# A new instruction list for an attention-and-MLP block: first loads on two queues, segment 0's Q and K in the space of w2 and hT, steps of VectorE on GpSimd

## The chip, the core and the metric

The kernel runs on one core of a Trainium2 chip. The core has TensorE (PE, matmuls), VectorE (DVE), ScalarE (ACT), GpSimd (POOL) and SyncE (SP), each with its own instruction stream executed in order, and 16 DMA engines that are fed by queues of SP and of ACT. Times are microseconds on the device. The metric is the time of one execution; the profile's span runs from its first to its last instruction.

## The reference

One layer on x of 2048 tokens by 640: attention with a compressive memory, then an MLP, each behind a layer norm and with a residual. All inputs are bfloat16.

```python
q, k, v = (heads(layernorm(x) @ w) for w in (wq, wk, wv))      # 32 heads of 20
for s in range(4):                                             # segments of 512 tokens
    p = softmax(q_s @ k_s.T * 20**-0.5 + causal_mask)
    a_dot = p @ v_s
    a_mem = (phi(q_s) @ M) / (phi(q_s) @ z + 1e-6)             # phi(t) = t + 1 if t > 0 else exp(t)
    o_s = sigmoid(beta) * a_mem + (1 - sigmoid(beta)) * a_dot
    M, z = M + phi(k_s).T @ v_s, z + sum(phi(k_s))
h = x + concat(o) @ wo
out = h + silu(layernorm(h) @ w1) @ w2                         # hidden width 1728
```

## The kernel before

**Tiling.** Tokens lie in 16 blocks of 128, four to a segment. A segment goes through these steps, named as in the list below; s is the segment, b the block, c a column group of five, g one of eight groups of four heads.

- `n1_st b` (DVE): mean and variance of a block, two statistics instructions and one aggregate (L711, L714). `n1_ra`, `n1_rb` (POOL): add epsilon (L720), power -0.5 (L725). `n1_ap` (DVE): subtract and multiply (L732) into one of four buffers `xn`. In segment 0 PE transposes it (`n1_tp`, L741) and ACT copies it (`n1_te`, L750); later segments use a transposing DMA (`n1_tr`, L756). `n2_...` is the same for the second norm.
- `v s i` (PE, L783) and `ve` (ACT or DVE): V of a block. `pr s c w` (PE, L817) and `qe`: a projection to Q (w=0) or K (w=1) and its copy into the tile `QK`. `re_wq c`, `re_wk c` rearrange the columns of wq and wk first (L682 on ACT, L684 on DVE). `vt` (SP, L857): 12 small DMAs that gather the last heads from `QK` into `QKV` (the virtual heads, groups 5 to 7). `ex`, `pha`, `phb`: phi of Q and K.
- `qk` (PE, L893), `e` (ACT, L904: the exponential, 768 or 1024 elements at a time), `mk` (POOL, L915: the causal mask on a diagonal part), `av` (PE, L936), `oe`, `tn`, `nm`, `ad`: scores, softmax and output of a group. In segment 0 each group is done in halves: `x` for its first two blocks, `ya` and `yb` for the last two.
- `kt` (transposing DMA), `mz`, `ma`, `mb`: the memory. `ot`, `wo` (PE, L1119), `rs`: output projection and residual.
- `h1` (PE, L1153; its last tile of 64 columns L1148), `th` (ACT, L1162), `s` (DVE, L1168), `h2` (PE, L1195), `o` (DVE, L1208): the MLP.
- `fill N` (PE, L604): N matmuls on a zero tile whose result nothing reads.

**Order.** Nothing is scheduled on the chip. A string `ORDER` lists every step by name, with the PSUM banks and buffers that it takes (`:4`) and, where there is a choice, its engine (`/A` ACT, `/D` DVE, `/G` POOL). The program emits the steps in that order, so each engine's stream is the list reduced to that engine. A tracker (`Tracker`) adds the semaphore waits that reads and writes need. An instruction whose input is late holds up all that stand behind it on its engine. Eight PSUM banks are shared; a `qk` takes four.

**Loads.** SP issues nearly all DMAs. x0 to x3 are the four blocks of segment 0; x4, x8 and x12 load four blocks each for the later segments. wq and wk go to the space of the MLP's tile `sT`. In the list x8 comes after the first `vt`. Each segment writes the same tiles `QK`, `QKV` and `xT`, so that segment 1's projections wait for segment 0's scores.

Of the kernel before, what the change touches and what calls it, by code (L numbers as in the profile page):

```python
# [6 lines left out]
ALU = mybir.AluOpType  # L7
# [340 lines left out]
SPLIT0 = ()  # L348
WH = [(0, 0), (0, 1), (1, 0), (1, 1)]
# [33 lines left out]
mk6yb_256 qk7ya0:4 th0_0_0:0 s0_7_0:0 tn4y:0 h1_0_8_0:3 e7ya0:2 nm4y:3 mz01:1 s0_0_0 mz04:0 e7ya2 ma01/D:2 phb101 kt10:0
kt03:1 h1_0_3_0:2 ma04/D:1 tn5y:1 th0_8_0:1 qk7yb0:4 th0_3_0:0 s0_8_0 av6y:0 e7yb0:0 s0_3_0 h1_0_1_0:3 nm5y:1 e7yb2
h1_0_12_0:2 th0_1_0:1 mk7yb_0 qk8a0:4 th0_12_0:0 pr110:1 e8a2:1 s0_12_0 s0_1_0 mm0 mk7yb_256 e8a0 mzc0 h1_0_10_0:2
qe110/D av7y:3 th0_10_0:1 vt19:0 qk8e0:4 s0_10_0 pr130:1 e8e2:0 vt16 oe6y/D:1 w_w2_3 n1_ap10:2 oe7y/D:0 e8e0 h1_0_5_0:2
pha121:0 qe130/D:0 w_w2_0 h1_0_11_0:3 th0_5_0:1 mk8e_0 qk8b0:4 s0_5_0 th0_11_0:0 tn7y:0 h1_0_6_0:1 e8b0:6 nm7y:3 mz03:2
ma03/D:4 s0_11_0 e8b2 h1_0_2_0:0 pha100:0 n1_ap8:1 h1_0_13_0:2 pha120:0 th0_2_0:1 qk9a0:4 mk8b_0 th0_13_0:0 pr131:3
s0_13_0 e9a2:4 mk8a_0 s0_2_0 mk8b_384 e9a0 h1_0_4_0:0 qe131/D n1_tr8:0 mk8e_256 h1_0_9_0:2 pha141:2 th0_6_0:1 mm3
th0_4_0:0 qk9b0:4 s0_6_0 mzc4 mzc6 ex100:1 mk9a_0 vt17 av8:3 s0_4_0 th0_9_0:1 mzc3 pha110:0 e9b2:3 h2_0_0:0 mm2 phb100  # L390
phb121 s0_9_0 mm9 pha111:1 mtb2 vt18 vt110 mzc9 mm8 e9b0 mm11 h2_0_1 oe8/D:0 mzc5 n1_tr10 ex141:1 mk9b_0 mm10 qk10a0:4
tn6y:3 h2_0_2 e10a2:5 phb141 mm1 vt11 nm6y:0 mzc2 n1_rb9 h2_0_3 e10a0 vt13 mb01:0 mm7 vt111 mzc1 qk10b0:4 mk9b_384 o0
h2_1_0:2 e10b2:2 ot3 mb00:0 e10b0 tn8:0 h2_1_1 n1_tr11 ex120:0 mk10b_0 nm8:2,1 qk10e0:4 ex111:1 h2_1_2 vt15 mk10b_384
phb111 n1_ap9:0 e10e2:1 mk10a_0 vt14 av9:0 e10e0 phb120 ot2 h2_1_3 oe9/A:0 ex110:0 mk10e_0 mk10e_256 qk11a0:4 kt12:1 o1
wo3:0 e11a0:6 pha130:0 mb02:0 phb110 e11a2 vt10 av10:2 rs3 n1_tr9 ex131:0 qk11b0:4 mk11a_0 oe10/D:1 tn9:0 e11b0:2
nm9:1,0 vt12 wo2:2 e11b2 ex130:1 mk11b_0 qk12a0:4 rs2 v20:0 e12a2:4 n2_st2:7 mzc7 e12a0 mzc8 mk11b_384 av11:2 pha131:0
n2_st3:1 ve20/A:1 qk13a0:4 mz12:3 e13a0:2 e13a2 v21:0 ma12 kt11:1 n2_ra3 phb130 n2_rb3 mzc11 mz10:3 n2_ra2 mzc10 ve21/A
n2_rb2 qk12b0:4 ma10 n2_ap3:1 ad8:0 e12b0:6 tn10:0 n2_tr3 pr210:3 nm10:0,1 mk13a_0 e12b2 mb03:0 qe210/A:0 ad9 qk12e0:4
oe11/D:1 pr220:0 e12e0:0 phb131 mk12b_0 n2_ap2:2 kt13:0 e12e2 mk12b_384 pr231:1 pha140:0 mk12a_0 qe220/A:0 n2_tr2
mk12e_0 qk13b0:4 qe231/D:0 tn11:2 e13b2:5 pr200:0 mk12e_256 nm11:3,0 ad10 e13b0 av12:1 qe200/D:0 mk13b_0 qk14a0:4 v23:2  # L400
e14a2:1 phb140 mk13b_384 oe12/D:1 mb04:0 e14a0 av13:1 ve23/A qk14b0:4 mz13:0 e14b2:3 pr221:2 ma13 oe13/D:0 e14b0
h1_0_7_1:3 qe221/A mk14b_0 qk14e0:4 th0_7_1:1 tn13:0 s0_7_1 mk14a_0 pr211:2 nm13:3,1 mk14b_384 e14e0:0 e14e2 h1_0_8_1:3
qe211/D mk14e_0 qk15a0:4 th0_8_1:1 pr241:0 e15a0:4 s0_8_1 mk14e_256 ad11 e15a2 av14:2 qe241/D:0 ad13 mz11:1 oe14/A:0
qk15b0:4 ma11 mk15a_0 e15b0:1 tn14:2 h1_0_4_1:1 nm14:3,1 e15b2 pr201:0 th0_4_1:1 mk15b_0 tn12:4 s0_4_1 qe201/A
h1_0_12_1:7 nm12:0,0 mk15b_384 qk16b0:0 e16b0:2 th0_12_1:0 ad14 av15:6 h1_0_13_1:4 ad12 oe15/D:0 e16b2 pr240:5 pha200:0
s0_12_1 th0_13_1:1 pha210:0 pha211:0 tn15:6 s0_13_1 qe240/A ex210:0 qk16a0:0 nm15:0,0 pr230:4 e16a2:6 e16a0 h1_0_10_1:5
# [54 lines left out]
def build(nc, es, A_x, A_wq, A_wk, A_wv, A_wo, A_beta, B_x, B_w1, B_w2, out):  # L461
# [229 lines left out]
    for c in range(NC):  # L691
        load_w(f"w1_{c}", w1_sb[:, c, :], B_w1[128 * c:128 * c + 128, :], -1 + 0.2 * c, 1.4, [(W["w1"], [c])])
# [172 lines left out]
    def declare_ticks(s):  # L865
# [5 lines left out]
        def operands(g, sub=WH):  # L871
            if g < 5:
                return (qk[g], sub), QK[:, g, 0, :], QK[:, g, 1, :]
# [395 lines left out]
```

## Time and profile before

| | |
|---|---|
| timed runs | 305.26, 305.55, 305.59 us; median 305.55 |
| profiled execution, first to last instruction | 303.6 us |
| median of the runs less that span | 1.95 us |
| PE, DVE, ACT, POOL busy | 294.4, 214.4, 226.6, 141.7 us |
| first V matmul starts | 9.03 us |
| first scores, first exponential (segment 0) | 16.33, 16.72 us |
| last scores of segment 0 | 67.47 us |
| DMA | 24.65 MB, mean 81 GB/s |

The profile's page gives busy time by engine, the span in 40 slices, the DMA queues, the chain that ended last, and the costliest groups of instructions; the trace adds timelines, waits and busy time by windows. In rows of groups the columns are line, engine, operation, output and input tiles with shapes, count, busy time, mean ns of one, and the idle time before them with what ended it. A line such as L711 is that line of the program before; the changed program's lines lie a few further on.

### The profile page before, as it was taken

To read this page: it belongs to the slowest core of one execution; us is meant where nothing else is said; L and a number is where in the kernel's file an instruction comes from. 1 tells how busy PE (TensorE), PEld (TensorE's weight loads), DVE (VectorE), ACT (ScalarE), POOL (GpSimd) and SP (SyncE) were. 2 spreads that over 40 slices of the span, in tenths; PEclk is the share of its full clock that TensorE was granted. 3 is DMA by queue.
4 is the path that set the end of the run, shared out by engine and by line. 5 is a ranking of instruction groups with operands and counts; after the bars stand their busy time and mean duration, and the time that the engine had idled before them with its cause. 6 is when DMAs were issued, how large, how long until landed. Compare 5 with 4: busy or idle time off the path is not lost.

```text
span 303.6 us, 7334 instructions
## 1 busy us (share of the span) xinstructions
PE 294.4 (97%) x2934; PEld 167.9 (55%) x2934; DVE 214.4 (71%) x492; ACT 226.6 (75%) x321; POOL 141.7 (47%) x280
## 2 busy tenths in 40 slices
PE   6999989999999999999999999999999999999996
PEld 5634545466565455566643545556564466764565
DVE  4888967877868866958588975858847494835623
ACT  3689988999999999899889989968779951004500
POOL 3346574532875856546847317564564730400000
PEclk9999999999999999999999999999999999999999
DMA  6938375843544130063551300043241006221003
GB/s 211 363 104 159 69 153 87 272 37 77 166 87 75 39 42 2 2 122 69 106 154 42 67 19 0 2 89 69 56 97 36 2 0 89 43 66 66 0 3 107
DMA packets 48721, 24.65 MB, mean 81 GB/s; under 512 B 39152, under 2 KB 47600, under 8 KB 48688
## 3 DMA queue, kind: packets, MB, share of 16 engines
q1 hardware_dynamic: 48400, 23.86, 34.6%
q8 instruction: 23, 0.38, 0.5%
q10 hardware_dynamic: 288, 0.33, 0.4%
q14 instruction: 10, 0.08, 0.1%
HBM read 10.41 MB, written 2.62 MB: 43 GB/s over the span
## 4 chain that ended last, share of the span: by engine, by line
PE 72%; ACT 12%; DVE 7%; DMA 4%; SPq 2%; issue 1%; POOL 0%; ACTq 0%
PE ps_all L1195 17%; PE ps_all L1153 13%; PE ps_all L817 13%; ACT PT L904 8%; PE ps_all L893 7%; PE ps_all L1119 6%; PE ps_all L783 5%; PE ps_all L936 5%; DVE sT L1168 3%; DMA wv_sb<-in_A_wv_dram 2%; ACT th L1162 2%; PE ps_all L965 2%; PE ps_all L1058 2%; DMA x_tok<-in_A_x_dram 1%; PE ps_all L969 1%
## 5 line engine op out<-in xcount | busy, mean ns | idle before, releaser
L904 ACT ACTIVATE PT<-ps_all 128x1024 bf16<-128x1024 f32 (+1 forms) x168 | 156.3, 985 | 16.9 <-PE ps_all L893 15.9
L915 POOL TENSOR_SCALAR_AFFINE_SELECT PT<-PT 128x512 bf16<-128x512 bf16 x128 | 81.5, 650 | 52.8 <-ACT PT L904 51.5
L1195 PE MATMUL ps_all<-w_sb,sT 128*128 128x320 bf16 (+2 forms) x462 | 64.8, 295 | 0.1
L1153 PE MATMUL ps_all<-hT,w_sb 128*128 128x512 bf16 (+1 forms) x325 | 62.5, 337 | 0.5 <-DVE sT L1168 0.4
L1162 ACT ACTIVATE th<-ps_all 128x512 f32<-128x512 f32 (+2 forms) x70 | 34.0, 505 | 35.1 <-PE ps_all L1153 24.6
L1168 DVE SCALAR_TENSOR_TENSOR sT<-th,ps_all 128x512 bf16<-128x512 f32 (+2 forms) x70 | 37.6, 558 | 23.8 <-ACT th L1162 23.2
L1195 PEld LDWEIGHTS ps_all<-w_sb,sT 128*128 128x128 bf16 x462 | 43.2, 98 | 18.5 <-issue 1.9
L1153 PEld LDWEIGHTS ps_all<-hT,w_sb 128*128 128x128 bf16 x325 | 29.8, 98 | 25.4 <-issue 2.1
L1010 POOL TENSOR_TENSOR otok<-on 128x320 bf16<-128x320 bf16 x24 | 19.2, 804 | 23.7 <-DVE on L1002 23.6
L711 DVE BATCH_NORM_STATS2 stt<-x_tok 128x6 f32<-128x320 bf16 x64 | 27.8, 476 | 3.4 <-DMA x_tok<-in_A_x_dram 3.2
L1208 DVE SCALAR_TENSOR_TENSOR x_tok<-ps_all,x_tok 128x640 bf16<-128x640 f32 (+3 forms) x18 | 13.3, 748 | 19.0 <-PE ps_all L1195 18.9
L720 POOL TENSOR_TENSOR rst<-mvt,eps_c 128x1 f32<-128x1 f32 x32 | 7.1, 223 | 40.4 <-DVE mvt L714 36.0
L817 PE MATMUL ps_all<-xT,wqr 128*128 128x512 bf16 x100 | 25.0, 381 | 0.0
L783 PE MATMUL ps_all<-wv_sb,xT 128*128 128x320 bf16 x160 | 24.4, 300 | 0.4 <-DMA wv_sb<-in_A_wv_dram 0.3
L817 PE MATMUL ps_all<-xT,wkr 128*128 128x512 bf16 x100 | 24.8, 380 | 0.0
L1119 PE MATMUL ps_all<-wo_sb,oT 128*128 128x320 bf16 x160 | 24.1, 299 | 0.4 <-DVE rd L996 0.2
L936 PE MATMUL ps_all<-PT,Vx 128*32 128x256 bf16 (+3 forms) x576 | 24.4, 287 | 0.0
L893 PE MATMUL ps_all<-QK 20*128 20x256 bf16 (+3 forms) x360 | 20.5, 286 | 1.0 <-ACT PT L904 0.7
L1002 DVE TENSOR_TENSOR on<-ps_all,rd 128x640 bf16<-128x640 f32 x24 | 19.8, 824 | 1.9 <-POOL otok L1010 1.1
L826 DVE CAST QK<-ps_all 128x512 bf16<-128x512 f32 x25 | 16.9, 684 | 5.1 <-PE ps_all L817 5.0
L1119 PEld LDWEIGHTS ps_all<-wo_sb,oT 128*128 128x128 bf16 x160 | 14.8, 97 | 8.1 <-issue 2.8
L783 PEld LDWEIGHTS ps_all<-wv_sb,xT 128*128 128x128 bf16 x160 | 14.7, 98 | 7.9 <-issue 1.5
(71 smaller groups left out, 329.4 us busy)
## 6 DMA issues: line engine op xcount, KB each, us to landing
out_dram<-x_tok SPq DMA_DIRECT2D x15, 160.0 KB, 1.9
w_sb<-in_B_w_dram SPq DMA_DIRECT2D x5, 432.0 KB, 4.5
x_tok<-in_A_x_dram SPq DMA_DIRECT2D x3, 640.0 KB, 5.3
w_sb<-in_B_w_dram SPq DMA_DIRECT2D x3, 480.0 KB, 3.8
QKV<-QK SPq DMA_DIRECT2D x16, 72.0 KB
wv_sb<-in_A_wv_dram SPq DMA_DIRECT2D x1, 800.0 KB, 7.2
sT<-in_A_wq_dram SPq DMA_DIRECT2D x1, 800.0 KB, 8.9
sT<-in_A_wk_dram SPq DMA_DIRECT2D x1, 800.0 KB, 10.6
```

The source lines that it names most:

```text
L711: T.add(DV, lambda e, hh=hh: e.bn_stats(out=stt[:, s, 6 * hh:6 * hh + 6], in_=xb[:, 320 * hh:320 * hh + 320]), reads=R((xa, xsub)), writes ...
L783: fns.append(lambda e, c=c, hh=hh: e.matmul(bank(ps, hh)[:, 0:320], lhsT=xT[:, c, 128 * i:128 * i + 128], rhs=wv_sb[:, c, 320 * hh:320 * h ...
L817: fns = [lambda e, kc=kc: e.matmul(bank(ps)[:, lo:hi], lhsT=wt[:, kc, c, :], rhs=xT[:, kc, lo:hi], start=(kc == 0), stop=(kc == NC - 1)) f ...
L893: fns.append(lambda e, j=j, o=o, r=r, q0=q0, q1=q1, qa=qa, ka=ka: e.matmul(ps_all[:, o:o + q1 - q0], lhsT=ka[32 * r:32 * r + DH, 128 * j:1 ...
L904: T.add(AC, lambda e: e.activation(out=pt[:, pta.slot, q0:q0 + 2, 0:width], in_=sc3[:, b0:b0 + 2, 0:width], func=ACT.Exp, scale=SCALE), re ...
L915: T.add(PO, lambda e: e.affine_select(out=v, in_=v, pattern=[[0, 4], [1, 128]], compare_op=ALU.is_ge, fill=0.0, base=0, channel_multiplier ...
L936: fns.append(lambda e, j=j, r=r, h=h, pa=pa, pt=pt, co=co, q0=q0, ji=ji: e.matmul(bank(po)[32 * r:32 * r + 32, q0:hi], lhsT=Vx[:, vx.slot, ...
L1119: fns.append(lambda e, c=c, hh=hh: e.matmul(bank(ps, hh)[:, 0:320], lhsT=oT[:, c, 128 * i:128 * i + 128], rhs=wo_sb[:, c, 320 * hh:320 * h ...
L1153: fns = [lambda e, c=c: e.matmul(bank(ps)[:, lo:hi], lhsT=w1_sb[:, c, 128 * f:128 * f + 128], rhs=hT[:, c, lo:hi], start=(c == 0), stop=(c ...
L1162: T.add(AC, lambda e: e.activation(out=th[:, tha.slot, lo:hi], in_=bank(ps)[:, lo:hi], func=ACT.Tanh, scale=0.5), reads=R((ps, [0])), writ ...
L1168: T.add(DV, lambda e: e.scalar_tensor_tensor(out=sT[:, f, lo:hi], in0=th[:, tha.slot, lo:hi], scalar=1.0, in1=bank(ps)[:, lo:hi], op0=ALU. ...
L1195: fns.append(lambda e, f=f, t0=t0, fr=fr, hh=hh, n=n: e.matmul(bank(pa, hh)[:, 0:n], lhsT=sT[:, f, t0:t0 + 128], rhs=w2_sb[:, fr, c0 + 320 ...
```

## The change

1. The first loads alternate between SP's and ACT's queue: x0, wv (first three of five row blocks), x2, wq on SP; x1, x3, wv (last two), wk on ACT. All of w1 is one DMA on ACT's queue right behind wk, not five on SP's. x8 is issued on SP behind x4, wo and the two ends of w2.
2. Segment 0's Q and K (`QZ`) and its virtual heads (`QZV`) lie in the space of `w2_sb`, and its transposed blocks in `hT`. The loads of w2 wait for the reads of these tiles. Segment 1 no longer shares a tile with segment 0 for them.
3. Epsilon's addition and the power become one step `r` (addition on POOL or DVE, power on POOL). The apply `ap`, and the first step of phi, `pha`, may run on POOL. In the new list POOL has 24 of 32 applies and 13 of 30 `pha`; DVE has 11 of 32 additions. ACT has 11 of 40 `oe` (17 before), 14 of 40 `qe` (15), 7 of 16 `ve` (5), 1 of 10 `re` (3).
4. The last tile of h1 runs as 20 matmuls of 32 columns rather than 10 of 64.
5. The list is new in whole. Fillers were 30, 8, 7, 6 and 10 matmuls; they are 54 (ahead of the first transpose) and 4.

```diff
-    load_x(1, 1, -99, 2.33, "fix", (SP,))
-    load_w("wv", wv_sb[:, :, :], cw(A_wv), -98, 4.96, [(W["wv"], [0])], "fix", (SP,))
-    load_x(2, 1, -97, 4.79, "fix", (AC,))
+    load_x(1, 1, -99, 2.33, "fix", (AC,))
+    load_x(2, 1, -97, 4.79, "fix", (SP,))
     load_x(3, 1, -96, 4.82, "fix", (AC,))
+    load_w("wv0", wv_sb[:, 0:3, :], cw(A_wv[0:384, :]), -98, 4.96, [(W["wv"], [0])], "fix", (SP,))
+    load_w("wv1", wv_sb[:, 3:5, :], cw(A_wv[384:640, :]), -98, 4.96, [(W["wv"], [1])], "fix", (AC,))
+    load_w("q", wraw[:, 0, :, :], cw(A_wq), -94, 6.58, [(sT0, ["q"])], "fix", (SP,))
+    load_w("k", wraw[:, 1, :, :], cw(A_wk), -93, 8.51, [(sT0, ["k"])], "fix", (AC,))
...
-    for c in range(NC):
-        load_w(f"w1_{c}", w1_sb[:, c, :], B_w1[128 * c:128 * c + 128, :], -1 + 0.2 * c, 1.4, [(W["w1"], [c])])
+    load_w("w1", w1_sb[:, :, :], cw(B_w1), -1, 7.0, [(W["w1"], range(5))], "plain", (AC,))
...
+    QZ = w2_flat[:, 0:10 * L].rearrange("p (c w t) -> p c w t", c=5, w=2)
+    QZV = w2_flat[:, 10 * L:16 * L].rearrange("p (c w t) -> p c w t", c=3, w=2)
...
-        G.task(f"{tag}ra{b}", {PO: 0.26}, e_rstd, [(st, ["mv"]), (C, ["eps"])], [(st, ["r"])], prio)
-        G.task(f"{tag}rb{b}", {PO: 0.56}, e_pow, [(st, ["r"]), (C, ["half"])], [(st, ["r"])], prio)
+        G.task(f"{tag}r{b}", {PO: 0.82, DV: 0.7}, e_rstd, [(st, ["mv"]), (C, ["eps", "half"])], [(st, ["r"])], prio)
...
-        G.task(f"{tag}ap{b}", {DV: 0.46}, e_apply, [(xa, xsub), (st, ["mv", "r"])], [(xn, [0])], prio)
+        G.task(f"{tag}ap{b}", {DV: 0.46, PO: 1.0}, e_apply, [(xa, xsub), (st, ["mv", "r"])], [(xn, [0])], prio)
...
-                            bank(ps)[64 * k:64 * k + 64, lo:hi], lhsT=w1_sb[:, c, 128 * f:FF],
-                            rhs=hv[:, c, k, b0 // 2:b1 // 2, :], start=(c == 0), stop=(c == NC - 1),
-                            tile_position=(0, 64 * k)) for c in range(NC) for k in range(2)]
+                            bank(ps)[32 * k:32 * k + 32, lo:hi],
+                            lhsT=w1_sb[:, c, 128 * f + 32 * (k % 2):128 * f + 32 * (k % 2) + 32],
+                            rhs=hv[:, c, k // 2, b0 // 2:b1 // 2, :], start=(c == 0), stop=(c == NC - 1),
+                            tile_position=(0, 32 * k)) for c in range(NC) for k in range(4)]
```

The new list by engine, up to the first outputs of segment 0:

```
SP    x0 w_wv0 x2 w_q beta x4 w_wo w_w2_4 w_w2_5 x8 n1_tr5 n1_tr6 vt06 vt00 vt09 kt00 vt03 kt01 vt08 vt07 ...
ACT   x1 x3 w_wv1 warm w_k w_w1 n1_te0 n1_te3 n1_te2 ve00 zf0 lsc0 ve03 n1_te1 re_wq3 ve02 qe011 ex011 qe010 e1x2 ...
DVE   zpad sel n1_st0 n1_st3 n1_r3 n1_ap0 n1_st2 n1_st1 n1_ap2 n1_ap1 re_wk0 re_wk1 re_wk4 re_wk2 re_wq0 re_wq1 zf1
      n1_st9 re_wq2 epsg1 lsc2 n1_r9 n1_st5 n1_st4 n1_st6 n1_ap5 n1_st8 re_wk3 n1_st11 n1_st7 n1_r11 pha011 re_wq4
      lsc3 pha001 phb011 phb001 qe031 qe041 pha021 qe030 ...
POOL  ... mzc6 (n1_r9) n1_r5 mzc3 n1_r4 n1_r6 n1_ap6 n1_ap4 n1_r8 n1_ap8 n1_r7 n1_ap7 mk1x_0 mk1x_256 mk0x_0 ...
PE    fill54 n1_tp0 fill4 n1_tp3 v00 n1_tp2 v03 n1_tp1 v02 pr011 pr010 pr001 qk1x0 pr000 pr021 qk0x0 pr020 v01 qk2x0
      pr031 pr041 qk0yb0 pr030 qk1yb0 pr040 av1x qk3x0 av0x qk4x0 tn0x tn1x v11 qk0ya0 av2x mz00 av3x tn2x qk1ya0
      av4x tn3x av0y tn0y qk5x0 ...
```

In the list before, DVE has the rearrangements of wq and wk by the steps n1_st6 and n1_st7, and n1_st9 behind the copies of V of segment 0 (29.1 us); POOL has its first mask between n1_ra6 and n1_rb6 (18.4 us).

277 lines of the change are left out of this document (146 added, 131 removed), and 1 row of the table pools.

## Prediction

> **What bounds the kernel now.** I read the page first, then busy time by windows, the chain, and the timeline of each engine over the first 70 us.
>
> ```profile
> PE 294.4 (97%) x2934; PEld 167.9 (55%) x2934; DVE 214.4 (71%) x492; ACT 226.6 (75%) x321; POOL 141.7 (47%) x280
> ```
>
> TensorE is busy 97% of the 303.6 us span, fillers included. A list that only reshuffles its work can win what lies around that: the time before the first real matmul, the fillers and the waits. Windows (us, then PE, PEld, DVE, ACT, POOL, clock, DMA share, GB/s):
>
> ```profile
> 2.00:4.00 2.00, 2.00 (x11) 1.44 (x10) 0.37 (x1) 1.99 (x2) 0.29 (x4) 1.00 0.91 313
> 4.00:9.00 5.00, 3.48 (x31) 2.58 (x29) 4.11 (x12) 0.97 (x2) 2.22 (x7) 1.00 0.91 287
> 9.00:17.00 8.00, 7.90 (x60) 4.53 (x61) 6.41 (x23) 5.15 (x13) 1.79 (x6) 1.00 1.06 354
> ...
> 16.30:67.50 51.20, 49.18 (x590) 26.08 (x593) 42.17 (x115) 46.74 (x68) 28.17 (x61) 1.00 0.57 124
> 67.50:303.60 236.10, 231.64 (x2257) 132.94 (x2256) 161.40 (x342) 171.73 (x239) 107.83 (x196) 1.00 0.27 58
> ```
>
> Two things are to be seen. From 9 to 17 us all 16 DMA engines are busy (1.06) at 354 GB/s: loads come no faster than that. And from 16.3 us (first scores, qk1x0) to 67.5 (last scores of segment 0, qk7yb0) PE and ACT are both nearly full, while afterwards PE alone sets the pace. So whatever segment 0 loses stays lost, since PE has no room later.
>
> Timeline, fillers and the first loads:
>
> ```profile
> 1.12 5.03 PE L604 MATMUL ps_all<-zpad 128*128 128x256 bf16 x30 [1.12 <-DVE zpad L583]
> ...
> 9.03 1.52 PE L783 MATMUL ps_all<-wv_sb,xT 128*128 128x320 bf16 x10 [0.35 <-DMA wv_sb<-in_A_wv_dram]
> ...
> 23.78 0.52 SPq L567 DMA_DIRECT2D x_tok<-in_A_x_dram  x1
> ...
> 30.47 0.93 PE L604 MATMUL ps_all<-zpad 128*128 128x256 bf16 x7
> ```
>
> The first V waits for wv. The load x8 (blocks 8 to 11) is issued at 23.78 us, when the queue is empty, and its first reader, at 29.1, hardly waits. Groups that price the moved steps:
>
> ```profile
> L915 POOL TENSOR_SCALAR_AFFINE_SELECT PT<-PT 128x512 bf16<-128x512 bf16 x128 | 81.5, 650 | 52.8 <-ACT PT L904 51.5
> L711 DVE BATCH_NORM_STATS2 stt<-x_tok 128x6 f32<-128x320 bf16 x64 | 27.8, 476 | 3.4 <-DMA x_tok<-in_A_x_dram 3.2
> L1010 POOL TENSOR_TENSOR otok<-on 128x320 bf16<-128x320 bf16 x24 | 19.2, 804 | 23.7 <-DVE on L1002 23.6
> L725 POOL TENSOR_TENSOR rst<-rst,eps_c 128x1 f32<-128x1 f32 x32 | 18.0, 562 | 1.0
> L732 DVE TENSOR_SCALAR xn_rot<-x_tok,mvt,rst 128x640 bf16<-128x640 bf16 x32 | 16.3, 518 | 3.4 <-POOL rst L725 3.4
> ```
>
> **The change part by part.** *Start.* In the trace 16 fillers start 0.213 us apart, up to 4.29 us, and the rest 0.108 us apart. Fifty-four therefore end at 4.29 + 38 x 0.108 = 8.4, plus about 0.2. Now they stand ahead of the first transpose, which is ready near 6.7. Transpose 0.45, copy by ACT 0.70: the first V starts at about 9.8, not 9.03. wv itself, 1440 KB in on two queues, lands before that. Loss 0.75.
>
> *Order to the first scores.* After that V: transpose, v03, transpose, v02, three projections (1.53 and 1.08 to 1.24 each, the ACT copies between) put qk1x0 at 18.4, where it was at 16.32. Two V's are done by then that stood at 26.7 and 28.5, so most of these 2.1 us comes back; PE's real work ahead of qk7yb0 is the same in both lists within 0.2 us.
>
> *Fillers.* The 23 in mid-run (0.93, 0.83 and 1.26 in the timeline) go. They stand where PE waits for ACT, so I count them only inside the stretch below.
>
> *x8 and the DVE queue.* This decides. SP now issues x8 right behind the first weights, and on DVE the statistics of block 9 (n1_st9), which need x8, stand ahead of the statistics of blocks 5, 4 and 6 and ahead of re_wq2, re_wk3, re_wq4 and the copies qe031, qe041 and qe030. Whatever is queued there waits for x8, and so do the projections pr020, pr031 and pr040 of segment 0.
>
> When does x8 land? In front of it or beside it lie x0 to x3 640 KB, wv, wq and wk 2400, x4 640, wo 800, two w2 ends 160, itself 640, and on the other queue all of w1, 2212: 7492 KB. By the windows 626 KB are in at 4.0 us; then five us at 287 (one queue) to 350, and the rest at 354 to 390 (estimate: the highest early slice on the page is 363, w1's rows are longer). That is 9 + 5431/354 = 24.3 or 9 + 5116/390 = 22.1. I take T = 23, since x8 is last on its queue and the two queues hold nearly equal bytes (3840 and 3652). If SP's queue ran alone the bound would be 2.2 + 3840/354 = 13; but with both queues loaded at the start neither was preferred (two x blocks each, 3.1 and 3.3 us from issue to landing in the issue table). The Trainium skill, "DMA: Bandwidth & Descriptors", section "Queues, rings and completion order", says that SP and ACT own one ring each on the same 16 engines, which take turns between rings packet by packet; by that x8 cannot overtake w1, and 23 stands; no run here shows two long queues together.
>
> From T, DVE by rows (two statistics and an aggregate start 1.03 apart, a rearrangement 0.35 to 0.5, a copy 0.6): block 9 T+1.0, re_wq2 T+1.4, blocks 5, 4, 6 T+4.85, block 8 T+6.3, re_wk3 T+6.8, blocks 11, 7 T+8.9, qe031 T+11.3, qe041 T+11.9, qe030 T+12.7. PE therefore starts pr020 at T+1.5, pr031 at T+6.9, qk1yb0 at T+11.4, pr040 at T+12.
>
> *POOL behind it.* POOL has the power step of block 9 in its queue too, then four of the applies it takes over, and only then the first mask. An apply of 640 elements on POOL is in no row. Bounds: 0.81 from the one-input mask (650 ns for 512), 1.6 from the two-input add (804 for 320). I take 1.0, nearer the mask, as only one input is a full tensor. Chain: power of 9 T+2.3; blocks 5, 4, 6 (0.66 each behind their statistics) T+5.6; two applies T+7.6; block 8 T+8.3; the third apply reuses a buffer and waits for the transposing DMA of block 5 (issue T+5.4, 2.7 us by the issue table), T+9.7; block 7 and a power T+10.9; fourth apply T+11.9. Then 14 masks 0.60 apart and one power, 8.95: av0y can start at T+20.95 = 43.95. Behind it ACT's copy and qk5x0 at 45.35, where it was 35.83. SP has the transposes of blocks 5 and 6, then two more and the 12 copies into the virtual-head tile (0.65 to 0.75 each) ahead of qk5x0: the last is issued at about 42.3 and lands 2.5 later, 44.8, so this cover is thin.
>
> *The ACT-paced stretch.* From qk5x0 to qk7yb0 ACT must start 16 exponentials of 768 (0.70 apart), 12 of 1024 (0.90), 5 plain ones (0.52), 5 tanh (1.3) and 3 copies (1.4): 27.3, with handovers 28.5 at least; the same stretch took 31.64 before, with a filler in it. I take 29.5. qk7yb0 is then at 74.85, against 67.47: 7.4 later. Nothing of it is made up, as ACT is full here and PE full afterwards.
>
> *The rest.* Afterwards the same PE work (+0.2) runs in 236.1 us. Waits over 0.15 us there sum to about 4.4 by the start times; the new list may halve or double some of them: 0, range -2 to +2. DVE gets rid of 24 applies (0.52) and 13 phi steps (0.33 to 0.41) and takes 11 additions; ACT has 6 copies fewer. Neither is what PE waits for after 67, so 0; if that cover were gone it would show as a loss in DVE, which has 30% free. The last tile of h1 in 20 matmuls of 32 columns rather than 10 of 64 streams the same 256 columns four wide; the 16-matmul attention groups of that shape take 0.66 us like the 0.67 of now: 0 to +0.4 each, five times, 0 taken. w2 must now wait for segment 0's scores. Its third part is issued after qk7yb0, the fourth after the third has landed, 3.8 us each by the issue table: 82.5. Behind them on SP stand segment 1's virtual-head copies, needed after 100. h2 stood at 81.4 and is now near 88.8: 0, up to 2 if a part comes late. Q and K of segment 1 in a second space: no gain, since pr141 and pr101 still come behind qk2yb0 in the list.
>
> Sum: 303.6 + 7.4 + 0.2 = 311.2 of span. The runs' median is 305.55 with the span at 303.6, so 1.95 lies around it: 313.1, I say 313.
>
> **Rivals.** *Faster: x8 is early.* If SP's queue gets ahead so that x8 lands early, nothing is held up. qk7yb0 stands at T+51.85 in the sum above, so the loss ends at T = 15.4; an undisturbed walk by the same rows gives av0y at 36.35, qk5x0 at 37.75 and qk7yb0 at 66.25 to 67.25; with 2 us fewer waits later, 300.6 to 303.6 of span, 302.5 to 305.5. For it: the loads start on two queues and the first window moves 313 already. Against: 7492 KB at 354. Chance 0.10 for faster, 0.02 for level.
>
> *Slower, but less: SP's queue gets more than half.* x8 at 19: four us off the main case, 309. For it: w1 is one long DMA that starts after ACT's table load and first activation, near 5. Chance 0.16.
>
> *Slower still: PE's clock falls back.* PE stands idle from 21.1 to T+1.5, over 3 us, and half idle up to 45; in the trace its longest idle time at the start is 1.2 us (6.15 to 7.36), after which matmuls ran at the fast spacing. The work there, about 13 us between pr020 and qk5x0, would take 26 at 0.213 per 256 columns, in 24 us of room: +2 to +5, 315 to 318. Chance 0.12. The Trainium skill, "TensorE: Matmul & The Clock Gate", section "What's actually happening", says so: the gate halves the clock after an idle window of about 3.4 us. The cold fillers up to 4.29 agree; no wait here is long enough to show the fall.
>
> **How the numbers follow.** Main case 0.60, at 313, its own range 310 to 315.5 (T 22 to 24.3, apply 0.8 to 1.6, later waits). With the rivals 8 in 10 lie in 306.5 to 318. Faster by over 0.2% (which is about what this measurement can tell) 0.10, level 0.02, slower 0.88.
>
> **What would show it.** Right: DVE waits some 8 us for x_tok's DMA before statistics near 23 us; PE idles before L817's projections in 21 to 37; first mask on POOL after 33; qk7yb0 near 74; PE full after it. Wrong: x8 landing before 17, masks by 25, or PE waits in mid-run that no DMA explains.

## The result and the profile after

The changed kernel takes 347.2 us (median of 347.0, 347.16 and 350.05); the kernel before took 305.4 beside it. A fourth run of 352.63 lies over 1.5% above the fastest and counts as slow; medians and ratios here leave out such runs. The ratio is 1.140 with an interval of 1.135 to 1.145. The direction was forecast, the size was not: 313 was said, with 318 as the upper end. The profiled execution took 347.16 us with a span of 345.4; the span before was 303.6, so 41.8 us have to be found.

First the page: busy time by engine, the chain that ended last by engine and by line, and the groups of the two steps that went to GpSimd, of the masks and of the statistics (the last two columns of a group are busy time with the mean ns of one, and idle time with what ended it).

```profile
PE 301.7 (87%) x2981; PEld 169.4 (49%) x2981; DVE 212.2 (61%) x476; ACT 223.2 (65%) x311; POOL 223.5 (65%) x306
...
PE 35%; POOL 31%; DVE 12%; DMA 9%; ACT 4%; SPq 3%; issue 2%; POOLq 1%; ACTq 1%; DVEq 0%
...
L933 POOL TENSOR_SCALAR_AFFINE_SELECT PT<-PT 128x512 bf16<-128x512 bf16 x128 | 81.7, 650 | 30.9 <-ACT PT L922 28.4
...
L747 POOL TENSOR_SCALAR xn_rot<-x_tok,mvt,rst 128x640 bf16<-128x640 bf16 x24 | 60.3, 2514 | 2.9 <-DMA hT<-xn_rot 1.0
...
L725 DVE BATCH_NORM_STATS2 stt<-x_tok 128x6 f32<-128x320 bf16 x64 | 28.0, 479 | 12.4 <-DMA x_tok<-in_A_x_dram 11.9
...
L856 POOL TENSOR_SCALAR phiK<-QK 128x512 bf16<-128x512 bf16 x8 | 15.6, 1944 | 8.0 <-DMA phiKt<-phiK 7.9
```

TensorE has the same work and is busy 87% of the time instead of 97%. GpSimd went from 141.7 to 223.5 us, and 31% of the chain that ended last runs through it. An apply takes 2514 ns there and a first step of phi 1944 ns (for K; 1921 for Q). On VectorE, in the kernel before, they took 518 and 333 to 405.

Next the windows up to the last scores of segment 0 (qk7yb0, 89.8 us) and behind them (us, then PE, PEld, DVE, ACT, POOL with instruction counts, clock, DMA share, GB/s):

```profile
18.40:89.80 71.40, 51.18 (x561) 24.43 (x560) 40.87 (x118) 49.33 (x71) 52.19 (x59) 0.86 0.37 77
89.80:345.40 255.60, 234.10 (x2306) 133.39 (x2298) 162.29 (x327) 163.99 (x223) 157.07 (x192) 0.99 0.27 52
```

Segment 0 ends 22.4 us later than before (67.5), and the part behind it takes 255.6 us where it took 236.1: 19.5 more, in a part for which the prediction put 0.2. Of the segment's first half, the timelines of SP's queue, VectorE, GpSimd and TensorE show this chain:

```profile
4.84 6.30 SPq L577 DMA_DIRECT2D w_sb<-in_B_w_dram  x2
11.19 2.68 SPq L574 DMA_DIRECT2D x_tok<-in_A_x_dram  x1
...
25.62 0.89 DVE L725 BATCH_NORM_STATS2 stt<-x_tok 128x6 f32<-128x320 bf16 x2 [9.90 <-DMA x_tok<-in_A_x_dram]
...
27.09 2.31 PE L834 MATMUL ps_all<-hT,wqr 128*128 128x512 bf16 x5 [5.80 <-DVE wqr L692]
...
31.37 5.06 POOL L747 TENSOR_SCALAR xn_rot<-x_tok,mvt,rst 128x640 bf16<-128x640 bf16 x2
...
41.30 2.50 POOL L747 TENSOR_SCALAR xn_rot<-x_tok,mvt,rst 128x640 bf16<-128x640 bf16 x1
43.76 4.58 POOL L933 TENSOR_SCALAR_AFFINE_SELECT PT<-PT 128x512 bf16<-128x512 bf16 x7
...
45.16 0.51 PE L954 MATMUL ps_all<-PT,Vx 128*32 128x256 bf16 x8 [6.35 <-POOL PT L933]
```

SP itself was held up while it issued: 6.3 us for the two ends of w2 and 2.7 for x8; what held it is not shown. VectorE waits 9.9 us for x8, and TensorE 5.8 us for the rearrangement that stands behind its statistics. Then four applies at 2.5 us hold the first mask until 43.8, and TensorE waits 6.35 us for it. At the other end the last h1 waits for the last apply and its transposing DMA:

```profile
301.80 2.50 POOL L747 TENSOR_SCALAR xn_rot<-x_tok,mvt,rst 128x640 bf16<-128x640 bf16 x1
...
307.25 2.29 PE L1172 MATMUL ps_all<-hT,w_sb 128*128 128x512 bf16 x5 [5.20 <-DMA hT<-xn_rot]
```

And TensorE's clock falls to half four times, here the first two and the last (same columns as the windows above; the third figure from the right is the clock):

```profile
24.30:27.10 2.80, 0.01 (x1) 0.01 (x1) 1.44 (x7) 0.00 (x0) 0.00 (x0) 0.50 0.02 7
27.10:31.10 4.00, 4.00 (x13) 1.81 (x14) 3.90 (x15) 1.11 (x2) 2.87 (x8) 0.50 0.01 2
...
45.10:51.50 6.40, 5.80 (x62) 2.48 (x62) 4.37 (x10) 4.14 (x7) 6.33 (x11) 0.50 0.67 69
...
307.20:311.00 3.80, 3.75 (x27) 1.43 (x28) 0.00 (x0) 0.81 (x2) 0.00 (x0) 0.50 0.26 88
```

### The profile page after: what moved, and what is told of

Its sections match the earlier page's. It is cut to its first block, busy times and chain, and to the rows that moved or that the text cites. A ratio compares the mean times of both kernels' runs of the same rounds, so it can differ in the third digit from the quotient of the medians.

```text
span 345.4 us, 7437 instructions
## 1 busy us (share of the span) xinstructions
PE 301.7 (87%) x2981; PEld 169.4 (49%) x2981; DVE 212.2 (61%) x476; ACT 223.2 (65%) x311; POOL 223.5 (65%) x306
## 4 chain that ended last, share of the span: by engine, by line
PE 35%; POOL 31%; DVE 12%; DMA 9%; ACT 4%; SPq 3%; issue 2%; POOLq 1%; ACTq 1%; DVEq 0%
POOL xn_rot L747 12%; PE ps_all L1214 9%; PE ps_all L1172 9%; POOL PT L933 7%; DMA x_tok<-in_A_x_dram 4%; POOL phiK L856 4%; PE ps_all L799 4%; PE ps_all L954 4%; PE ps_all L834 3%; POOL rst L741 3%; PE ps_all L911 3%; POOL phiQ L856 3%; ACT PT L922 3%; DMA oT<-otok 2%; DVE sT L1187 2%
## 5 line engine op out<-in xcount | busy, mean ns | idle before, releaser
L1172 PE MATMUL ps_all<-hT,w_sb 128*128 128x512 bf16 (+1 forms) x325 | 65.2, 347 | 9.2 <-DMA hT<-xn_rot 8.0
L1181 ACT ACTIVATE th<-ps_all 128x512 f32<-128x512 f32 (+2 forms) x70 | 33.9, 507 | 49.4 <-PE ps_all L1172 34.9
L747 POOL TENSOR_SCALAR xn_rot<-x_tok,mvt,rst 128x640 bf16<-128x640 bf16 x24 | 60.3, 2514 | 2.9 <-DMA hT<-xn_rot 1.0
L725 DVE BATCH_NORM_STATS2 stt<-x_tok 128x6 f32<-128x320 bf16 x64 | 28.0, 479 | 12.4 <-DMA x_tok<-in_A_x_dram 11.9
L1227 DVE SCALAR_TENSOR_TENSOR x_tok<-ps_all,x_tok 128x640 bf16<-128x640 f32 (+3 forms) x18 | 13.4, 746 | 34.8 <-PE ps_all L1214 34.8
L741 POOL TENSOR_TENSOR rst<-rst,eps_c 128x1 f32<-128x1 f32 x32 | 18.2, 573 | 20.7 <-DVE rst L735 19.1
L969 DVE TENSOR_SCALAR oTs<-ps_all,lsc 128x512 bf16<-128x512 f32 (+1 forms) x29 | 17.8, 618 | 18.1 <-PE ps_all L954 17.4
L954 PEld LDWEIGHTS ps_all<-PT,Vx 128*32 128x32 bf16 x576 | 12.5, 97 | 25.5 <-POOL PT L933 9.0
L799 PE MATMUL ps_all<-wv_sb,xT 128*128 128x320 bf16 x120 | 19.6, 314 | 2.2 <-DMA xT<-xn_rot 1.3
L856 POOL TENSOR_SCALAR phiK<-QK 128x512 bf16<-128x512 bf16 x8 | 15.6, 1944 | 8.0 <-DMA phiKt<-phiK 7.9
L834 PE MATMUL ps_all<-xT,wkr 128*128 128x512 bf16 x75 | 18.7, 380 | 0.0
```

Of the source, the lines that this page charges most:

```text
L747: T.add(eng, lambda e: e.tensor_scalar(out=xn_rot[:, xn.slot, :], in0=x_tok[:, b % 12, :], scalar1=mvt[:, s, 0:1], scalar2=rst[:, s, :], o ...
L799: fns.append(lambda e, c=c, hh=hh: e.matmul(bank(ps, hh)[:, 0:320], lhsT=xT_[:, c, 128 * i:128 * i + 128], rhs=wv_sb[:, c, 320 * hh:320 * ...
L834: fns = [lambda e, kc=kc: e.matmul(bank(ps)[:, lo:hi], lhsT=wt[:, kc, c, :], rhs=xT_[:, kc, lo:hi], start=(kc == 0), stop=(kc == NC - 1)) ...
L856: T.add(eng, lambda e: e.tensor_scalar(out=o, in0=QK_[:, c, w, :], scalar1=0.0, scalar2=1.0, op0=ALU.max, op1=ALU.add), reads=R((qk[c], wa ...
L954: fns.append(lambda e, j=j, r=r, h=h, pa=pa, pt=pt, co=co, q0=q0, ji=ji: e.matmul(bank(po)[32 * r:32 * r + 32, q0:hi], lhsT=Vx[:, vx.slot, ...
L1172: fns = [lambda e, c=c: e.matmul(bank(ps)[:, lo:hi], lhsT=w1_sb[:, c, 128 * f:128 * f + 128], rhs=hT[:, c, lo:hi], start=(c == 0), stop=(c ...
```

## The experiments

Theory A: the price of the steps on GpSimd is the term that failed. Theory B: the order of the new list loses the time. Theory C: x8's wait does. The fallen clock was the fourth suspect. The table has all runs but the probe (329.7 us in its one run; its added instructions lie in the way of the end): median and ratio to the kernel before with its interval, then the profiled span, the start of the last scores of segment 0 in it, and what is left behind that. The spans are of one execution each; those of e4 alone go from 319.6 to 324.4 us, so differences of a few us between spans are rough. "Narrow" kernels (e4, e5, e8, e9, e12, e13, e15, e16) leave out part of the computation.

| kernel | us | ratio, interval | span | segment 0 | behind it |
|---|---|---|---|---|---|
| before | 305.4 | | 303.6 | 67.5 | 236.1 |
| after | 347.2 | 1.140, 1.135–1.145 | 345.4 | 89.8 | 255.6 |
| e1 steps back on VectorE | 344.9 | 1.128, 1.123–1.133 | 340.9 | 87.7 | 253.2 |
| e2 w1 behind x8 | 342.4 | 1.121, 1.118–1.124 | 339.9 | 84.4 | 255.5 |
| e3 both | 339.8 | 1.108, 1.100–1.115 | 338.1 | 84.5 | 253.6 |
| before with the steps on GpSimd | 353.0 | 1.156, 1.154–1.158 | 350.4 | 81.1 | 269.3 |
| e4 narrow steps | 323.3 | 1.060, 1.055–1.066 | 322.9 | 86.0 | 236.9 |
| e5 narrow, w1 behind | 319.1 | 1.047, 1.045–1.049 | 317.7 | 81.0 | 236.7 |
| e8 the same with fillers | 318.7 | 1.045, 1.042–1.049 | 316.2 | 78.7 | 237.5 |
| e9 e5 with VectorE's order | 316.6 | 1.036, 1.029–1.042 | 313.9 | 77.1 | 236.8 |
| e15 e9 spread, fillers | 312.1 | 1.023, 1.020–1.027 | 310.3 | 73.6 | 236.7 |
| e16 e15 without fillers | 312.6 | 1.026, 1.022–1.029 | 311.1 | 73.5 | 237.6 |
| e10 repaired, complete | 331.1 | 1.085, 1.079–1.091 | 327.5 | 81.3 | 246.2 |
| e12 narrow applies only | 327.9 | 1.072, 1.067–1.078 | 326.2 | 84.5 | 241.7 |
| e13 narrow phi steps only | 342.8 | 1.125, 1.123–1.128 | 340.9 | 91.9 | 249.0 |
| e14 last four applies back | 342.1 | 1.123, 1.117–1.129 | 341.4 | 91.9 | 249.5 |
| e7 before, two queues | 305.2 | 1.001, 1.000–1.003 | 303.7 | 67.9 | 235.8 |
| e11 before, fewer fillers | 305.4 | 1.002, 1.000–1.004 | 303.6 | 67.1 | 236.5 |

### e1, e2, e3: undoing whole parts

```diff
# e1: every apply and phi step off GpSimd, an apply one or two VectorE steps later
-n2_r14/D n2_ap14/G:2 n2_tr14:0 wo12:3 rs12 n2_st12:7 ... pha131/G:2
+n2_r14/D wo12:3 rs12 n2_st12:7 n2_ap14/D:2 n2_tr14:0 ... pha131/D:2
# e2: w1 on SP's queue, behind x8
-    load_w("w1", ..., range(5))], "plain", (AC,))
+    load_w("w1", ..., range(5))], "plain", (SP,))
# e3: both
```

> All 24 applies and 13 first phi steps that the changed kernel has on GpSimd go back to VectorE (an apply behind the next one or two VectorE steps), nothing else changes; x8 still lands near 25 us. Theory A (GpSimd's price: 2.51 us an apply and 1.94 a phi step against 0.52 and 0.33 to 0.41 on VectorE): the masks of segment 0 start some 8 us earlier and the last scores of segment 0 come at 77 instead of 89.8, later segments and the last h1 lose nothing more: 316 us (312 to 321), POOL busy near 142. Theory B (the new list's own order loses the time): over 330. Theory C (x8's wait carries most): over 335, because that wait is still there.

> w1 is issued on SP's queue behind x8 instead of on ACT's queue beside it; GpSimd keeps its steps. x8 should land near 16 us and VectorE's wait of 9.9 us go. Theory A: segment 0 gains 7 to 10 us, the rest (GpSimd's price) stays: 339 us (336 to 342). Theory C: 320 or less. Theory D (GpSimd bounds segment 0 anyway, so the wait is covered): 345 or more.

> Both edits together: no apply or phi step on GpSimd, and w1 behind x8. Theory A with the x8 wait: nothing large is left, 306 us (302 to 311); TensorE busy over 96% again. Theory B: over 320.

The times are 344.9, 342.4 and 339.8 us. By the bounds as put, theory A missed all three, e2 by only 0.4 us; theory B's conditions (over 330, over 320) were met in e1 and e3, and theory C's in e1 but not in e2. Taking the steps off GpSimd brought GpSimd back to 142 us of busy time and gave only 2.3 us in the median. With w1 behind it x8 was used at 20.3 instead of 25.6 us, not at 16, and segment 0 ended 5.4 us earlier. That does not decide for theory B, because e1 and e3 changed more than the price. The first row is from e2, the others, from VectorE in e3, show why the steps did not pay when they went home:

```profile
20.28 0.89 DVE L723 BATCH_NORM_STATS2 stt<-x_tok 128x6 f32<-128x320 bf16 x2 [4.17 <-DMA x_tok<-in_A_x_dram]
...
91.73 0.42 DVE L1185 SCALAR_TENSOR_TENSOR sT<-th,ps_all 128x256 bf16<-128x256 f32 x1 [0.54 <-ACT th L1179]
103.00 0.29 DVE L854 TENSOR_SCALAR phiK<-QK 128x512 bf16<-128x512 bf16 x1 [10.85 <-DMA phiKt<-phiK]
```

The phi step pha131 needs a buffer that a transposing DMA (kt14) must have read, and that DMA stands on SP's queue behind w2's parts, which wait for segment 0's scores, and 11 of the 12 copies of virtual heads. On GpSimd the step waited 7.9 us. On VectorE the wait for that DMA, 10.85 us here, stops the steps for which TensorE waits: TensorE stood for 10.3 us. So e1 and e3 took a price away and put a wait in its place; they do not measure the price.

### The price in the old list

```diff
-        G.task(f"{tag}ap{b}", {DV: 0.46}, ...        # and T.add(DV, ... in the emitter
+        G.task(f"{tag}ap{b}", {DV: 0.46, PO: 1.0}, ...   # T.add(eng, ...; pha the same
-n1_ap6:1 ... pha121:0       (24 applies and 13 phi steps of the old list)
+n1_ap6/G:1 ... pha121/G:0
```

> The kernel before, its list and loads, with only the same 24 applies and 13 first phi steps put on GpSimd where they stand. Theory A: GpSimd's busy time goes from 141.7 to some 223 us, masks and powers stand behind it, 327 us (318 to 335), an apply near 2.5 us. Theory B or C (list or loads carry the loss): under 312.

It took 353.0 us, beyond the range: 46.8 us of span, with loads and order as they were before the change. So moving the steps, at their real price, is enough for all of the loss in a list that was not made for it. The loss lies elsewhere, though: 13.6 us up to the last scores of segment 0 and 33.2 behind them, where the new list loses 22.4 and 19.5. So it does not show that it is the loss in the new list.

### e4, e5: the steps at the price that was assumed

```diff
+            n = 256 if eng == PO else D          # pha: 184 of 512
-            ... out=xn_rot[:, xn.slot, :], in0=x_tok[:, b % 12, :],
+            ... out=xn_rot[:, xn.slot, 0:n], in0=x_tok[:, b % 12, 0:n],
```

> The changed kernel with each apply on GpSimd cut to its first 256 of 640 columns and each phi step on GpSimd to 184 of 512, so that they cost about the 1.0 and 0.7 us that the prediction and the program's cost table give them (the other columns keep a zero written at the start, so part of the computation is left out); order, waits and loads as they are. Theory A (the price of these steps is the term that failed): with x8 at 25.6 the prediction's sum gives 316 us (312 to 321). Theory B (the order of the new list loses the time whatever the steps cost): over 328.

> The same narrow steps, and w1 on SP's queue behind x8. Theory A: price and x8 together are the whole loss: 308 us (303 to 313). Theory B: over 320.

e4's windows up to and behind the last scores of segment 0, and its group of applies:

```profile
18.80:86.00 67.20, 52.17 (x564) 24.95 (x564) 41.18 (x118) 49.14 (x71) 41.35 (x61) 0.87 0.38 78
86.00:322.90 236.90, 231.28 (x2303) 133.00 (x2298) 160.09 (x327) 163.60 (x224) 126.22 (x189) 1.00 0.28 56
...
L746 POOL TENSOR_SCALAR xn_rot<-x_tok,mvt,rst 128x256 bf16<-128x256 bf16 x24 | 29.9, 1248 | 5.1 <-DMA hT<-xn_rot 3.2
```

Here the loads and the whole order stay, and the steps get shorter; the columns left out keep zeros, which three added instructions on VectorE write at the start (1.9 us in sum). 22.5 us of span go (23.9 in the median), 18.7 of them behind segment 0, where 236.9 us are left against 236.1 before. That part is thereby explained but for 0.8 us, with the waits and the falls of the clock that the long steps bring about. The narrow apply still took 1.25 us and the narrow phi step 0.85, so 22.5 is less than what lies between the real price and the assumed one. The times are above the expectation of A (323.3 for 312 to 321, 319.1 for 303 to 313), and below those of B (328, 320): theory A holds for the part behind segment 0, and segment 0 has a loss of its own.

### e6: what makes the price

```diff
+ for each of: two operations, per-partition scalars; two, constants; one, scalar; one, constant; two on 320
+     T.add(eng, lambda e: e.tensor_scalar(out=wkr[0:n], in0=wqr[0:n], scalar1=a, scalar2=b, ...))
+ T.add(PO, tensor_copy 640); T.add(PO, tensor_tensor 640)
```

> The kernel before, with two rounds of single GpSimd instructions on idle tiles near 285 us, and the same on VectorE: tensor_scalar on 640 columns with two operations and per-partition scalars, with two operations and constants, with one operation of either kind, two operations on 320 columns, a copy and a two-input add of 640. If two operations make the price: 2.5, 2.5, then 0.8 to 1.3 for one operation, 1.25 for 320. If any tensor_scalar costs 3.9 ns a column on GpSimd: 2.5 for all of 640. The two-input add should take 1.6 (2.5 ns a column).

The second of the two rounds on GpSimd, in the order of the edit, and the first two instructions on VectorE, from the timelines:

```profile
278.94 2.50 POOL L1233 TENSOR_SCALAR wkr<-wqr,eps_c 128x640 bf16<-128x640 bf16 x1
281.53 2.35 POOL L1233 TENSOR_SCALAR wkr<-wqr 128x640 bf16<-128x640 bf16 x1
283.98 1.88 POOL L1233 TENSOR_SCALAR wkr<-wqr,eps_c 128x640 bf16<-128x640 bf16 x1
285.95 1.81 POOL L1233 TENSOR_SCALAR wkr<-wqr 128x640 bf16<-128x640 bf16 x1
287.86 1.44 POOL L1233 TENSOR_SCALAR wkr<-wqr,eps_c 128x320 bf16<-128x320 bf16 x1
289.37 0.72 POOL L1237 COPY wkr<-wqr 128x640 bf16<-128x640 bf16 x1
290.17 1.39 POOL L1238 TENSOR_TENSOR wkr<-wqr 128x640 bf16<-128x640 bf16 x1
...
291.60 0.45 DVE L1233 TENSOR_SCALAR wkr<-wqr,eps_c 128x640 bf16<-128x640 bf16 x1 [20.32 <-POOL wkr L1238]
292.07 0.33 DVE L1233 TENSOR_SCALAR wkr<-wqr 128x640 bf16<-128x640 bf16 x1
```

Neither expectation fits: one operation instead of two saves a quarter, constants instead of scalars 0.1 to 0.2, and half the columns cost 1.44; an estimate from 2.50 and 1.44 is 0.4 us fixed and 3.3 ns a column. VectorE stood still from 271.3 to 291.6, throughout this round, and the first row has the duration that an apply has in the kernel (2.51), so the price is the instruction's own and not a contention with VectorE. The two-input add of 640 takes 1.39, less than the one-input step.

### e8, e9, e15, e16: segment 0

```diff
# e8 (on e5): fillers where TensorE idled
+fill20:7 (ahead of pr020) fill20:7 (pr031) fill14:7 (av1x) fill7:7 (av0x) fill6:3 fill5:7 fill6:7 fill18:6 (h1_0_3_0)
# e9 (on e5): VectorE's order
-re_wq1/D fill54:0 ... n1_st9:1 mzc10 re_wq2/D epsg1 lsc2 mzc6 n1_r9/D n1_st5:6 ...
+re_wq1/D re_wq2/D re_wk3/D re_wq4/D fill54:0 ... n1_st5:6 ... n1_st9:1 n1_r9/D n1_st8:6 ... n1_st10:0
# e15 (on e9): statistics of blocks 9, 8, 11, 10 ahead of qk5x0, qk6x0, qk7x0, qk2ya0, and fill8, 6, 5, 6, 14
# e16: e15 without these fillers
```

> The kernel with narrow steps and w1 behind x8, and fillers of 20, 20, 14, 7, 6, 5, 6 and 18 matmuls where TensorE stood idle in segment 0 (ahead of pr020, pr031, av1x, av0x, tn0y, qk6x0, wo1, h1_0_3). In it the granted clock was 0.5 at 27 to 31.8, 38 to 41.7, 48 to 51.6 and 75.5 to 79.9 us. If the fallen clock costs what it takes from TensorE there (half of about 15 us of work): 312.5 us (311 to 315), no window below 1.0. If ACT and GpSimd pace that stretch anyway: 317 or more. The narrow steps leave part of the computation out, as before.

> The kernel with narrow steps and w1 behind x8, and in the list the last three rearrangements (re_wq2, re_wk3, re_wq4) right behind the first six, and the statistics of x8's blocks 9, 8 and 11 (with their additions and block 8's apply) behind segment 0's projections. If the order of VectorE's queue makes the two holes ahead of pr020 and pr031 (2.1 and 2.3 us) and the first fall of the clock: 313.5 us (311.5 to 316). If it is not that: 318 or more.

> All steps narrow, w1 behind x8, the three rearrangements early, the statistics of blocks 8 to 11 one block each between the scores of groups 5, 6, 7 and 2y instead of in a bunch ahead of segment 0's output copies, and fillers of 8, 6, 5, 6 and 14 where TensorE idled. If bunch and clock are the rest of segment 0's loss: 309 us (306 to 312), last scores of segment 0 near 71. If the list's number of steps there (ACT's exponentials) paces it: 314 or more.

> e15's kernel without its five fillers: narrow steps, w1 behind x8, early rearrangements, statistics of blocks 8 to 11 spread. If the spread statistics made e15's gain: 312 us (310.5 to 313.5), with at most one short fall of the clock. If the fillers made it by holding the clock: 315 to 317, clock 0.98.

e8 kept the clock at 1.00 through the four windows in which e5 had lost it (it fell once elsewhere, from 43.9 to 47.3), and its segment 0 is 2.3 us shorter; the median moved by 0.4 us, and the intervals overlap. That is e8's second case (317 or more). e15 and e16 differ by the fillers alone, 312.1 and 312.6. So fillers that keep the clock up gain next to nothing here. The fillers take TensorE's time themselves, so the price of the fall alone is not measured, and that ACT and GpSimd pace the stretch is argued, not shown. e9 gave 2.5 us and stayed 0.6 above its range, and the spread of the statistics 4 more (e9 to e16): these are the waits of segment 0's own copies behind statistics of blocks that are needed tens of us later. e15 missed its range by 0.1 us and e16 is within its own. In e15 segment 0 still ends 6.1 us later than before, 2.6 of it by the first scores (in e16 6.0 and 1.8); the rest was not settled.

### e10 to e14, e7: repairs and parts

```diff
# e10: e3's engines and w1, e9's order, on SP: kt10 kt14 w_w2_3 ... (kt14 was eight entries behind kt10, w_w2_3 ahead of both)
# e12, e13: e4 for the applies alone, for the phi steps alone
# e14 (on after)
-n2_ap14/G:2 ... n2_ap12/G:0 ... n2_ap15/G:1 ... n2_ap13/G:3
+n2_ap14/D:2 ... n2_ap12/D:0 ... n2_ap15/D:1 ... n2_ap13/D:3       (each with its n2_tr behind it)
# e7 (on before): SP x0 wv0 x2 wq, ACT x1 x3 wv1 wk      # e11 (on before): fill7, fill6, fill10 out
```

> A complete kernel: the changed one with all applies and phi steps on VectorE, w1 behind x8, VectorE's order as in the run before, and on SP's queue kt14 right behind kt10 with w2's last part behind both (mz04 and ma04 moved up for it), so that no phi step waits for the transposing DMA that stood behind the virtual heads' copies (10.9 us in the run with both edits). Theory: that wait, the holes ahead of pr020 and pr031 and the clock they cost are what is left: 317 us (309 to 323) for 339.8. Rival: VectorE with 24 applies and 13 phi steps more is now the bound: 328 or more.

> The changed kernel with only the 24 applies on GpSimd narrow (256 of 640 columns, the rest a zero), phi steps whole. With all steps narrow 25 us went. By busy time the applies hold 24 x 1.5 = 36 of 52 us, and the end (h1 of the last segment waiting for the last apply) is theirs alone: 331 us (327 to 335). If the phi steps, which stand between masks, carry most: 340 or more.

> The changed kernel with only the 13 phi steps on GpSimd narrow (184 of 512 columns, the rest a zero), applies whole. By the same shares: 341 us (337 to 346). If phi carries most: 333 or less.

> The changed kernel, complete, with only the applies of the second norm of blocks 12 to 15 back on VectorE, behind the next one or two VectorE steps. h1 of the last segment waits 5.2 us for the last apply and its transposing DMA and then runs at half clock for 4 us: 341 us (339.5 to 343). If another input is late there: 346 or more.

> The kernel before with only the start of the change: x0, wv's first part, x2 and wq on SP, x1, x3, wv's second part and wk on ACT, w1 and all else where they were. If the start is bound by the first x block: statistics begin 1 us earlier (3.8 for 4.8) and the first V near 8.2 instead of 9.0, 304.9 us (304.4 to 305.4). If later waits swallow it: 305.4 to 305.7.

> The kernel before without its three fillers in mid-run (7, 6 and 10 matmuls). If they only fill waits for ACT, as the prediction took them: 305.4 us, at most 0.5 either way, clock 1.0. If they hold the clock up: one or two falls and 307 to 311 us.

e12 and e13 divide the price: 19.3 us of the median for the applies, 4.4 for the phi steps, together 23.7, what e4 took away (23.9). e14 shows the end: with four applies back the last h1 starts right behind the matmul before it, and the median falls by 5.0 us:

```profile
295.99 8.86 PE L1212 MATMUL ps_all<-w_sb,sT 128*128 128x320 bf16 x64
304.95 1.24 PE L1170 MATMUL ps_all<-hT,w_sb 128*128 128x512 bf16 x5
```

These three, e7 and e11 came within their ranges. e10 repairs e3 by 8.7 us but stays at 331.1, above its range, where its rival (328 or more) put it. VectorE is busy for only 68% of the span; but the moved steps, at places meant for another engine, wait there for transposing DMAs (8.2 us before phi steps, 4.7 before an apply), and TensorE's longest waits, 2.2 to 3.4 us, are for VectorE. Which of them costs what was not followed further. e7 begins its first V 1.1 us earlier (7.9) and its first scores as before (16.3): wq, which shares the DMA engines now, is first used at 12.04 instead of 11.13. e11's fillers are free, as the prediction took them, though without them the clock fell once, from 33.5 to 36.9. No run came below the kernel before.

## Why the prediction was wrong, point by point

- **The price of an apply on GpSimd** is the step that failed. It was taken as 1.0, between bounds of 0.81 (mask) and 1.6 (two-input add); it is 2.51, outside both. The bounds came from other kinds of instruction, scaled by columns, and the probe shows that at equal columns the kind of instruction makes the difference: at 640 columns 0.72 for a copy, 1.39 for a two-input add, 2.50 for this step. The first step of phi was not priced on GpSimd at all. e4 puts what follows at 22.5 us or more of the 41.8, 18.7 of them behind segment 0.
- **The 0 for the moved steps behind 67 us** fell with it. Near the assumed price the sum was right: 236.9, 236.7 and 236.7 us in e4, e5 and e15, for the 236.3 that was put. The prediction looked for a loss in VectorE only, not in GpSimd's queue; but masks, powers and applies share that queue, and GpSimd, idle for 35% of the span, still made TensorE wait 7.6 us for masks in segment 0, 2.5 behind it, and 5.2 for the last apply's block.
- **The h1 of the last segment** was not looked at. Its four applies are in series on GpSimd at the end, where nothing stands in for them: 5.0 us of the median (e14). This is part of the 18.7.
- **x8 and VectorE's queue** were right as a mechanism. T came at 25.6, behind the bounds of 22.1 to 24.3; pr020 (T+1.5), pr031 (T+6.9), qk1yb0 (T+11.4) and pr040 (T+12) each started within 0.1 us of their formula. The count of bytes was a little low, as w1's 2212 are thousands of bytes and the other loads units of 1024; in one unit the same bounds are 22.4 and 24.7. In the trace all but 0.03 MB was in by 24.0; the last 30 packets came between 24.0 and 25.7. As the prediction had it, x8 came last; the rate was not steady on the way: 292 GB/s from 9 to 13 us, 408 from 13 to 18, and 282 from 20.5 to 24.0, when w1 was in and SP's queue was alone. So "no faster than 354" did not hold. From 13 to 18 us the two queues did not share equally. In the rows of DMA queues for that stretch (packets, MB, share of the engines' time) ACT's queue with w1 has nearly three times the bytes of SP's:

```profile
q10 hardware_dynamic: 430, 1.49, 73.2%
q1 hardware_dynamic: 428, 0.54, 29.2%
```

  Packets are equal in number, 430 and 428, and unequal in size: 1.49 MB in 430 packets are some 3460 bytes each, a row of w1, and 0.54 MB in 428 some 1260, a row of SP's loads. The Trainium skill, "DMA: Bandwidth & Descriptors", section "Queues, rings and completion order", says that the engines take turns by packets; the trace agrees, and the prediction used the rule and forgot the sizes. They put w1 ahead; when the last load lands depends on the sum of the bytes and the rate. The rival "SP's queue gets more than half" went the other way in this stretch.
- **The chain on GpSimd** to the first mask had the right links, but for the wait of the third apply for a transposing DMA, which does not show behind the longer applies. At four applies 1.5 us longer each it gives T+17.9, that is 43.5, and the mask started at 43.76; the dropped wait makes the closeness partly luck. (T+11.9 and 8.95 are T+20.85, not T+20.95.)
- **The ACT-paced stretch** was put at 29.5 us. It took 34.8 (qk5x0 at 55.07 to qk7yb0 at 89.82), and 33.8 even in e15. ACT was busy 29.5 of the 34.75 in the trace, against 27.3 counted, so its work alone filled the 29.5; that it would run almost without gaps was wrong. What makes the gaps in e15 was not settled.
- **The clock** fell, as the rival said. It was priced at 2 to 5 us; fillers against it gain 0.4 and 0.5 in the median (e5 and e8, e16 and e15), 1.5 and 0.8 in the span. In the changed kernel it fell for longer (mean clock 0.960, in e5 0.979), so its price there stays open.
- **The start** was near in number: first V 10.3 for 9.8, first scores 18.41 for 18.4. But it was not the fillers that set the first V: TensorE waited 0.85 us, to 10.05, for block 3's apply on GpSimd. That the scores came on time all the same is partly luck. Fillers (e11) and w1's tail in 32 columns (3.15 us for its five groups before, 3.64 after, the last at half clock) were rightly put near nothing; the second space for Q and K, put at nothing, was not tested. w2's wait was put at nothing too, up to 2 if a part came late: TensorE did not wait for w2, but SP's queue behind it delayed kt14, which is the wait that came out in e3.
- **Faster because x8 is early** did not come: x8 was late. e5, with x8 in use at 21.4, does not test it, as the rival's loss ends at 15.4. In e15 and e16 VectorE shows no wait for x8 in segment 0, and the last scores come at 73.6 and 73.5, where the rival put 66.25 to 67.25.
- **The signs named beforehand:** VectorE's wait for x8, TensorE's idle time before projections and a first mask after 33 came. The last scores near 74 and a TensorE full behind them did not (89.8, and 234.1 of 255.6 us busy), and TensorE waited in mid-run for GpSimd, which had been named as a sign of being wrong.

Together, in spans of one execution each and taken in this order: 22.5 us for the price (e4), 5.2 for x8 (e5), 6.6 for VectorE's order (e16), and 7.5 that remain, 6.0 of them in segment 0 with its start, not settled.

## What to carry to other kernels

A step that goes to another engine needs a row of the same kind of instruction on that engine; where there is none, a probe of a few instructions costs one run, and bounds from other kinds of instruction can miss on the side that hurts. An engine with idle time is no free room when its queue also carries steps that the bound engine waits for: ask what stands behind the moved step, and look at the end of the program, where nothing covers. Narrowing a step in place measures its price without moving its waits; moving it back does not, because its waits move with it.

## What was not expected of the hardware

- GpSimd's price depends on the kind of instruction: 640 columns of bfloat16 cost 0.72 us as a copy, 1.39 as a two-input add, 1.81 to 1.89 as a one-operation and 2.35 to 2.52 as a two-operation tensor-scalar step, where VectorE takes 0.33 to 0.45 for the last two. VectorE's statistics were not slowed by 82 us more of GpSimd: they took 476 ns before and 479 after.
- TensorE's clock changes on a grid. In the changed kernel it fell at 24.3, 41.4, 85.7 and 304.2 us and came back at 31.1, 51.6, 89.1 and 311.0; all of these lie whole multiples of 3.41 us apart. In the 3.41 us before each fall TensorE was busy for 0.42, 0.86, 1.58 and 1.28 us, in those before each return for 3.38 us or more. Where the line lies is open: in e2 a stretch of the grid with 1.35 us of work (25.4 to 28.8) brought no fall, and in the kernel before with the steps on GpSimd one with 2.5 (49.4 to 52.8) did. The fall at 85.7 came 1.6 us after work had resumed. The Trainium skill, "TensorE: Matmul & The Clock Gate", section "What's actually happening", gives an idle window of about 3.4 us that runs freely; the trace agrees with the grid, but a window need not be wholly idle.
